# Tail V loads into freed K buffers and smaller V offsets in a grouped-query decode attention kernel

## Chip, cores, metric

One core of a Trainium2 chip. The time is device microseconds of one execution, quoted as a median of several. "TensorE" is the matrix engine (PE in the profile; PEld its weight loads), "ScalarE" is ACT, "VectorE" is DVE, "GpSimd" is POOL; SP is the engine that issues all loads. The "granted clock" is the share of TensorE's full clock that the profile records; in these traces it is 1.0 or 0.5 ("half clock") at any moment, and a mean over a run lies between (0.964 in the kernel before).

## The reference

One token of 32 query heads reads 8 K/V heads of 65,536 keys with 128 elements each, in bf16:

```python
B, Hq, Hkv, Sq, Sk, D = 1, 32, 8, 1, 65536, 128
k = jnp.repeat(k, Hq // Hkv, axis=1); v = jnp.repeat(v, Hq // Hkv, axis=1)
scores = jnp.einsum("bhqd,bhkd->bhqk", q, k) * D ** -0.5
p = softmax(scores, axis=-1)
out = jnp.einsum("bhqk,bhkd->bhqd", p, v)
```

K and V together are 268 MB, read once.

## The kernel before

A chunk is 8,192 keys (2 MB). Each head has 8 K chunks and 8 V chunks. For a K chunk, TensorE transposes 64 tiles into PSUM, the memory in which this kernel lets its results land ("TR"), VectorE evacuates (copies out) six and ScalarE two of its eight PSUM groups, and 64 score matmuls follow one chunk later ("QK"). ScalarE copies the scores out. After a head's last QK come its maximum and four exponentials on ScalarE (one for each query head), and only then can its V chunks be multiplied ("PV", 64 matmuls per chunk). An offset says how many K chunks of the next head pass before a head's first PV:

```python
    T=64, NK=4, NV=5,          # tiles per chunk, K buffers, V buffers
    DOFF=2, DOFF_LAST=1,       # offsets: heads 0-5, heads 6-7
...
        def merged(vdelay, vdelay_last):
            ...
            for (_, h, c) in kitems:
                lst.append((NCH * h + c, 0, ("K", h, c)))
            for (_, h, c) in vitems:
                d = vdelay_last if h >= H - 2 else vdelay
                lst.append((NCH * (h + 1) + c + d + 0.5, 1, ("V", h, c)))
            lst.sort(key=lambda x: (x[0], x[1]))
```

This one list orders both the loads and TensorE's work. A K load waits for the transposes of the K chunk four earlier, a V load for the PV five earlier.

ScalarE's program has the four exponentials in a row, between its evacuations:

```python
            for g_ in range(R):
                ac.activation(pview[:, g_, :], sview[:, g_, :], AF.Exp, ..., accum_out=...).then_inc(exp_done, 1)
```

## Time and profile before

| | before |
|---|---|
| time, median of 6 runs (range) | 662.66 us (658.25 to 668.54) |
| span of the profiled run | 660.0 us |
| TensorE busy | 601.2 us (91%), mean granted clock 0.964 |
| VectorE, ScalarE busy | 282.6 us, 198.6 us |
| transfers in the plateau (slices 5 to 36) | 423 to 427 GB/s |
| instruction fetches on the DMA engines (queue q8) | 97 packets, 1.59 MB |

The slices of the page cut the span into 40 parts. TensorE and the transfers both look full, so the busy shares alone can't say which of them sets the time; the waits can. The prediction shows these lines and reads them.

### The profile page before, as it was taken

The page shows a single profiled execution, that of the slowest core. Times are in us where ns is not written, and L with a number is a line of the kernel's source. Part 1 is how long each engine was busy: PE and PEld are TensorE (multiplying, and loading weights), DVE is VectorE, ACT ScalarE, POOL GpSimd, SP SyncE. Part 2 cuts the span into 40 slices and gives each one's busy share as a digit, 9 for nine tenths or more (in the row PEclk, how much of TensorE's full clock was granted, in tenths as well). Part 3 has the DMA queues.
Part 4 walks back from the last instruction along what each step waited for, and adds up shares of the span by engine and source line. Part 5 has one row for each costly group of instructions (what it writes and reads, how often), then busy time and mean ns, then how long its engine had stood idle before and what let it go on. Part 6 is the DMA issues. An engine that isn't in the chain of part 4 may idle for free.

```text
span 660.0 us, 25999 instructions
## 1 busy us (share of the span) xinstructions
PE 601.2 (91%) x12289; PEld 585.6 (89%) x12289; DVE 282.6 (43%) x491; ACT 198.6 (30%) x266; POOL 7.1 (1%) x22
## 2 busy tenths in 40 slices
PE   3889799889999999999999899999999999998998
PEld 3889699889989899898998889998899989898997
DVE  1767534344444435435434354354444444442300
ACT  1434522134222422226222162222522143221400
POOL 0000000000000000000000000000000000000000
PEclk9989798998999989999989999899999999998799
DMA  8999999999999999999999999999999999998694
GB/s 353 422 390 402 426 426 425 424 427 425 426 424 424 423 425 426 426 426 424 425 424 425 426 425 425 425 425 425 424 425 426 425 425 424 426 425 329 255 424 197
DMA packets 18621, 270.11 MB, mean 409 GB/s; under 512 B 2132, under 2 KB 2132, under 8 KB 2132
## 3 DMA queue, kind: packets, MB, share of 16 engines
q1 hardware_dynamic: 18516, 268.46, 96.5%
q8 instruction: 97, 1.59, 1.0%
q14 instruction: 8, 0.07, 0.0%
HBM read 268.44 MB, written 0.01 MB: 407 GB/s over the span
## 4 chain that ended last, share of the span: by engine, by line
PE 85%; issue 8%; ACT 3%; DMA 2%; DVE 1%; POOL 0%; POOLq 0%; DVEq 0%
PE trb L285 35%; PE pvb L327 35%; PE qkb L305 16%; ACT pts L445 2%; DMA vbuf<-in_v_dram 2%; ACT ktb L469 1%; DVE hpart L370 0%; ACT scs L421 0%; POOL hmaxa L250 0%; DVE hmax L377 0%; ACT negb L430 0%; DVE orows L400 0%; POOL ident L244 0%; POOL ident L242 0%; PE trb L264 0%
## 5 line engine op out<-in xcount | busy, mean ns | idle before, releaser
L360 DVE COPY ktb<-trb 128x1024 bf16<-128x1024 bf16 x384 | 237.9, 683 | 194.9 <-PE trb L285 193.6
L327 PE MATMUL pvb<-vbuf,pts 128*4 128x128 bf16 x4096 | 257.0, 226 | 19.6 <-issue 19.0
L327 PEld LDWEIGHTS pvb<-vbuf,pts 128*4 128x4 bf16 x4096 | 243.5, 88 | 24.2 <-issue 22.3
L285 PE MATMUL trb<-ident,kbuf 128*128 128x128 bf16 x4096 | 249.2, 222 | 17.0 <-issue 9.8
L285 PEld LDWEIGHTS trb<-ident,kbuf 128*128 128x128 bf16 x4096 | 234.9, 99 | 26.8 <-issue 12.6
L469 ACT ACTIVATE ktb<-trb 128x1024 bf16<-128x1024 bf16 x128 | 131.2, 1025 | 358.9 <-PE trb L285 358.9
L305 PE MATMUL qkb<-qT,ktb 128*128 128x4 bf16 x4096 | 113.8, 165 | 9.1 <-issue 9.1
L305 PEld LDWEIGHTS qkb<-qT,ktb 128*128 128x128 bf16 x4096 | 110.3, 96 | 10.2 <-issue 10.1
L370 DVE TENSOR_REDUCE hpart<-scs 128x4 f32<-128x256 f32 x64 | 38.7, 605 | 111.9 <-ACT scs L421 111.9
L445 ACT ACTIVATE pts<-scs,negb 128x512 bf16<-128x512 f32 x32 | 41.1, 1435 | 0.3
L421 ACT ACTIVATE scs<-qkb 128x256 f32<-128x256 f32 x64 | 24.5, 383 | 48.1 <-PE qkb L305 48.1
L400 DVE TENSOR_SCALAR orows<-pvb,rcol 4x128 bf16<-4x128 f32 x8 | 2.7, 339 | 57.4 <-PE pvb L327 57.4
L264 PE MATMUL trb<-ident,qsb 32*128 32x32 bf16 x1 | 0.2, 178 | 10.6 <-POOL ident L244 10.6
L264 PEld LDWEIGHTS trb<-ident,qsb 32*128 32x128 bf16 x1 | 0.1, 100 | 10.6 <-issue 10.6
L250 POOL PARTITION_ALL_REDUCE hmaxa<-hmax x8 | 3.0, 373 | 565.8 <-DVE hmax L377 565.8
L445 ACT ACTIVATION_READ_ACCUMULATOR pts<-scs,negb 128x1 f32 x32 | 8.2, 256 | 0.0
L430 ACT ACTIVATE negb<-hmaxa 128x4 f32<-128x4 f32 x8 | 1.6, 205 | 11.1 <-POOL hmaxa L250 11.1
L339 DVE CAST identf<-ident 4x4 f32<-4x4 bf16 x1 | 0.2, 158 | 10.5 <-POOL ident L244 10.5
L255 POOL PARTITION_ALL_REDUCE lsum<-rsum x8 | 3.4, 430 | 44.0 <-ACT pts L445 44.0
L411 ACT ACTIVATE dscr<-ident 128x1 f32<-128x1 bf16 x1 | 0.2, 202 | 8.5 <-POOL ident L244 8.5
L377 DVE TENSOR_REDUCE hmax<-hpart 128x4 f32<-128x32 f32 x8 | 1.7, 207 | 0.3
L411 ACT ACT_TABLE_LOAD x1 | 1.3, 1283 | 0.7 <-PEq L495 0.7
(11 smaller groups left out, 4.3 us busy)
## 6 DMA issues: line engine op xcount, KB each, us to landing
kbuf<-in_k_dram SPq DMA_DIRECT2D x64, 2048.0 KB, 20.6
vbuf<-in_v_dram SPq DMA_DIRECT2D x64, 2048.0 KB, 26.0
qsb<-in_q_dram SPq DMA_DIRECT2D x1, 8.0 KB, 1.7
out_dram<-orows SPq DMA_DIRECT2D x1, 8.0 KB
```

What stands on the lines that cost most here:

```text
L250: g.partition_all_reduce(hmaxa[:, h * R:(h + 1) * R], hmax[:, h * R:(h + 1) * R], P, bass.bass_isa.ReduceOp.max,).then_inc(hmaxa_rdy, 1)
L255: g.partition_all_reduce(lsum[:, h * R:(h + 1) * R], rsum[:, h * R:(h + 1) * R], P, bass.bass_isa.ReduceOp.add,).then_inc(lsum_rdy, 1)
L285: ins = pe.transpose(trb[bnk][:, (gti % TB) * P:(gti % TB + 1) * P], kv3[:, t, :], ident[:, :],)
L305: ins = pe.matmul(qkb[bnk][:, t * R:(t + 1) * R], lhsT=ktb[slot][:, t * P:(t + 1) * P], rhs=qT[:, h * R:(h + 1) * R], start=True, stop=True,)
L327: ins = pe.matmul(pvb[bnk][0:R, 0:D], lhsT=pts[pslot][:, tau * R:(tau + 1) * R], rhs=vv3[:, t, :], start=(tau == 0), stop=(tau == TPH - 1),)
L360: dv.tensor_copy(ktb[slot][:, j * TB * P:(j + 1) * TB * P], trb[bnk][:, :],).then_inc(tr_fre[bnk], 1)
L370: dv.tensor_reduce(hp[:, pslot, c, :], scs[pslot][:, c * T * R:(c + 1) * T * R].rearrange("p (t g) -> p g t", g=R), AX.X, ALU.max,).then_i ...
L377: dv.tensor_reduce(hmax[:, h * R:(h + 1) * R], hp[:, pslot, :, :].rearrange("p c g -> p g c"), AX.X, ALU.max,).then_inc(hmax_rdy, 1)
L400: dv.tensor_scalar(orows[:, h * D:(h + 1) * D], pvb[bnk][0:R, 0:D], rcol[:, h:h + 1], None, ALU.mult,).then_inc(pv_fre[bnk], 1)
L421: ac.activation(scs[pslot][:, qc * T * R:(qc + 1) * T * R], qkb[bnk][:, 0:T * R], AF.Copy,).then_inc(qk_fre[bnk], 1)
L445: ac.activation(pview[:, g_, :], sview[:, g_, :], AF.Exp, bias=negb[:, h * R + g_:h * R + g_ + 1], scale=scale, accum_out=rsum[:, h * R + ...
L469: ac.activation(ktb[slot][:, j * TB * P:(j + 1) * TB * P], trb[bnk][:, :], AF.Copy,).then_inc(tr_fre[bnk], 1)
```

## The change

The intent is to close the hole in the transfers near the end. Once no K is left to load, the K buffers that fall free take V chunks 0 to 3 of the last head, and both offsets shrink by one so that V comes earlier. Two further switches in the diff (FSPLIT, QKPV) are off and are cut here.

```diff
-    DOFF=2,
-    DOFF_LAST=1,
+    DOFF=1,
+    DOFF_LAST=0,
+    TAILK=1,
...
+    nkd = min(NK, NCH - 1) if TAILK else 0
+    for (_, h, c) in vitems:
+        if h == H - 1 and c < nkd:
+            kc_prev = NKC - NK + c
+            vdest[(h, c)] = ("k", kc_prev % NK, kc_prev)
+        else:
+            vb_idx[(h, c)] = cnt_vb
+            vdest[(h, c)] = ("v", cnt_vb % NV)
+            cnt_vb += 1
...   # SP, for a V chunk whose destination is a K buffer
+                    grp_last = kc_prev * GPB + (GPB - 1)
+                    sp.wait_ge(tr_full[grp_last % NTB], tr_full_after(grp_last))
+                    sp.dma_start(kbuf[kslot][:, :], src).then_inc(k_rdy[kslot], 16)
...   # TensorE reads V from there
+                    pe.wait_ge(k_rdy[kslot], 16 * (krdy_count(kslot, kc_prev) + vuses))
+                    vsrc = kbuf[kslot]
```

## The prediction

> **What bounds the kernel now.** The kernel streams 64 K chunks and 64 V chunks of 2 MB each. For each K chunk TensorE makes 64 transposes (L285) and 64 score matmuls (L305), for each V chunk 64 output matmuls (L327). Both streams leave on one queue, in the order in which TensorE uses them. I first read the page's slices, because 268 MB make the transfers the first suspect.

> ```profile
> PE   3889799889999999999999899999999999998998
> ...
> PEclk9989798998999989999989999899999999998799
> DMA  8999999999999999999999999999999999998694
> GB/s 353 422 390 402 426 426 425 424 427 425 426 424 424 423 425 426 426 426 424 425 424 425 426 425 425 425 425 425 424 425 426 425 425 424 426 425 329 255 424 197
> ```

> The transfers run flat at about 425 GB/s, except in slices 1 to 4 and in slices 37 and 38 (594 to 627 us), the hole that the change is aimed at. The windows view of 595 to 630 us reads 338, 334, 311, 298, 324, 170 and 305 GB/s in steps of 5 us. Against 425 that lacks (87+91+114+127+101+255+120) x 5 us = 4.5 MB, or 10.5 us of transfer. A naive reading makes that the gain. So the second view is the one of waits: does TensorE ever wait for a transfer?

> ```profile
> PE pvb L327 <- issue: 19.0, 20, 1.3
> ...
> PE trb L285 <- issue: 9.8, 16, 1.4
> ...
> PE qkb L305 <- issue: 9.1, 13, 1.2
> ...
> PE trb L285 <- ACT ktb L469: 6.7, 4, 3.7
> ...
> PE pvb L327 <- DMA vbuf<-in_v_dram: 0.5, 1, 0.5
> ```

> The columns are total us, times, longest. After its start TensorE waited for data once, for 0.5 us. Its idle time is 10.6 us before the first transpose, 37.9 us of short "issue" gaps, 6.7 us for ScalarE's evacuations and this 0.5 us. Together with 601.2 us busy that is 656.9 of the 660.0 us span; 2.4 us of what is left is the store at the end (last matmul 657.55). So TensorE is the bound and the queue runs ahead of it: K chunk 63 was issued at 571.58 us, a K chunk lands 20.6 us after issue (median), and its transposes started only at 610.58 us, some 18 us after it lay there. The margin isn't large: from one head's exponentials to the next (149.29, 226.97, 304.55 us) TensorE took 77.6 us for 8 pairs, 9.70 us a pair, while two chunks at 425 GB/s take 2 x 2.097 / 0.425 = 9.87 us.

> The third view is TensorE's timeline of the tail (start, duration):

> ```profile
> 614.16 1.64 PE L305 MATMUL qkb<-qT,ktb 128*128 128x4 bf16 x60
> 616.73 0.25 PE L305 MATMUL qkb<-qT,ktb 128*128 128x4 bf16 x4 [0.92 <-issue]
> 617.17 1.85 PE L305 MATMUL qkb<-qT,ktb 128*128 128x4 bf16 x64 [0.20 <-issue]
> 618.95 34.35 PE L327 MATMUL pvb<-vbuf,pts 128*4 128x128 bf16 x576
> 653.80 3.73 PE L327 MATMUL pvb<-vbuf,pts 128*4 128x128 bf16 x64 [0.50 <-DMA vbuf<-in_v_dram]
> ```

> After the last scores TensorE multiplies ten V chunks without a hole: nine in 34.35 us, 0.50 us for the last chunk, then that one. The hole in the transfers is inside TensorE's own busy time. Also to be seen: the first two of the ten (V of head 6) hide the exponentials of head 7.

> The fourth view is what those exponentials cost; the chain of waits shows it bare at head 0, where no V work lies in between:

> ```profile
> 66.27 0.39 ACT scs L421
> ...
> 66.69 0.61 DVE hpart L370
> ...
> 67.32 0.22 DVE hmax L377
> ...
> 67.67 0.40 POOL hmaxa L250
> ...
> 68.09 0.21 ACT negb L430
> ...
> 69.53 3.92 ACT pts L445 x7
> 73.45 0.86 ACT ktb L469
> ```

> The last score matmul ended at 66.25, the exponentials at about 73.45: 7.2 us from a head's last scores to its probabilities. I take the last matmul of head 7 (618.95) as a check: there ScalarE's last exponential starts at 624.74 and takes 1.42, so 626.2, again 7.2 us.

> [...] head 0's stall of 3.71 us and head 1's of only 1.19 us (150 to 154 us) are both followed by half clock, in the column before the DMA share:

> ```profile
> 77.00:80.50 3.50, 3.50 (x38) 3.50 (x35) 2.59 (x4) 0.38 (x1) 0.00 (x0) 0.50 1.01 431
> ...
> 155.60:159.00 3.40, 3.40 (x58) 3.38 (x55) 0.84 (x4) 0.61 (x2) 0.00 (x0) 0.50 0.99 414
> ```

> In such a stretch 64 matmuls take 5.3 us instead of 3.67, so a stall costs its own length plus about 1.7 us per stretch; after head 0's stall there were two stretches (73.7 to 80.5 us). [...] the evacuation at 73.45 waited behind four exponentials. [...]

> **The change part by part.**
> FSPLIT=1 and QKPV=0 switch their new code off: nothing.
> TAILK: V chunks 0 to 3 of head 7 go into the four K buffers as the transposes of K 60 to 63 release them. V chunks 4 to 7 need only V chunks 3 to 6 of head 6 to be consumed. No load of head 7 waits any more for an output matmul of head 7, or for one behind its exponentials. Estimate of the new tail, from the end of K 63's transposes (T): at the latest five chunks are then still to be issued, about 2 + 5 x 4.93 = 27 us, while TensorE's last chunk starts about 3.3 + 7.2 + 7 x 3.6 = 36 us after T. The last load gets about 9 us of slack. What it takes off the path is the 0.5 us wait.
> DOFF 2 to 1: V of heads 0 to 5 moves one pair earlier. The order of instructions on TensorE shows that head 0's first V multiply comes after K 9 instead of K 10, and that from a head's last scores to its first V multiply there is now one pair instead of two. One pair is enough: the transposes in it need ScalarE's evacuation, which stands behind the exponentials, so the wait is paid there as before (3.7, 1.2, 1.2, 0.6 us at four heads). Change: 0.
> DOFF_LAST 1 to 0, head 6: after the last scores of head 6 come V chunk 7 of head 5 and then at once chunk 0 of head 6, with no transposes between. 3.6 us of work against 7.2 us leaves a new stall of 3.6 us. In the kernel before, a whole pair lay there and head 6 had no stall of this kind (its exponentials ended at 547.1, TensorE went on). The half clock after it adds 1.7 to 3.4 us. Sum 5.3 to 7.0; one gap of 0.6 us (37.9 us over 64 pairs) may fall inside it. About 6.
> DOFF_LAST, head 7: after the last scores one V chunk of head 6 instead of two. Now the end follows 7.2 us of exponentials, then 8 chunks of 3.6 us = 28.8, plus 1.7 to 3.4 us of half clock: 37.7 to 39.4 us after the last scores. Before it was 657.55 - 618.95 = 38.6 us, with one chunk (3.6 us) more in it, which now lies ahead of the last scores. So 2.7 to 4.4 more, 0.5 us for the vanished load wait already in it. About 3.
> The sum is -0 (transfers) + 6 (head 6) + 3 (head 7) = +9 us at full effect. The clock part is uncertain, since half clock also follows chance gaps and part of it is there in the tail already; I shade to +7: 662.66 + 7 = 669.7.

> **The rivals.**
> (a) The transfers bind, the hole is real, and filling it gives up to 10.5 us: 652. For it: the flat 425 GB/s, 9.87 against 9.70 us a pair, and the last load landing 0.04 us before its matmul. Against: one wait of 0.5 us in 650.
> (b) The earlier V makes TensorE wait for loads in the middle, as the lead of some 18 us is lost. Queue and TensorE have the same order in both kernels, so the lead stays; against it also that V starts earlier in the slices where the queue has room. If so, 680.
> (c) The stalls come but the half clock doesn't, or it takes the place of half clock already there: +4, 667.
> (d) The gaps called "issue", 49 of them, shift with the new order. They depend on how the instructions fall, and could move the total by some 5 us either way.

> **Range and chances.** The six runs before spread from 658.25 to 668.54, so the median itself is good to some 3 us. With +2 to +12 for the stalls I say 661 to 676. Over 2% slower (above 675.9) needs both stalls with full half clock and bad luck in (d): 0.10. Over 2% faster (below 649.4) needs more than rival (a) can give: 0.04.

> **What would show each step.** Right: the slices lose the hole at 594 to 627 us, the last load lands some 9 us before the last matmul starts, and TensorE has no wait for DMA; two new waits of 2 to 4 us of L382 (the output matmul) on ScalarE's exponentials, one near 555 us and one about 35 us before the end, each with half clock after it. Wrong: no such waits, or the last matmul still waiting for its load, or a total number of half-clock stretches far below the 13 of the kernel before.

## More of the kernel before

In the PV multiply the probabilities are the stationary operand and V moves (in the page the weight load is 128x4, the matmul 128x128):

```python
                    ins = pe.matmul(
                        pvb[bnk][0:R, 0:D],
                        lhsT=pts[pslot][:, tau * R:(tau + 1) * R],
                        rhs=vv3[:, t, :], ...)
```

## The result

| | before | after |
|---|---|---|
| median (range; runs) | 662.66 us (658.25 to 668.54; 10 runs) | 671.04 us (664.86 to 673.91; 5 runs) |
| span of the profiled run | 660.0 us | 670.0 us |
| TensorE busy, mean clock | 601.2 us, 0.964 | 609.0 us, 0.954 |

The ratio is 1.0123, with a 95% interval from 1.0065 to 1.018. A ratio is the mean time of one kernel's fast runs over that of the other's fast runs of the same rounds, so it isn't quite the ratio of the medians. The change makes the kernel about 8 us slower, within the class "within 2%".

The page of the changed kernel, slices:

```profile
PE   3988799899999999999999989999999997999998
...
PEclk9998799988899999888899999999899988989889
DMA  8999999999999999999999999999999999998690
GB/s 354 424 409 426 427 423 428 425 423 426 425 426 423 425 425 425 425 425 426 424 423 416 404 424 418 425 426 421 429 423 425 425 424 407 425 399 315 269 410 5
```

The hole near the end hasn't gone. It reads 399, 315, 269 in slices 36 to 38, because loads into K buffers wait for transposes just as K loads do (SP's four such waits are 40.5 us together). But the last slice moves 5 GB/s instead of 197: the transfers are over well before TensorE is. In the trace the last V chunk landed at 654.6 us and was multiplied from 663.9 us, so it lay there for 9.3 us. In the kernel before, it landed as TensorE reached it.

The waits of TensorE in the changed kernel (total us, times, longest):

```profile
PE pvb L382 <- issue: 24.9, 23, 3.6
...
PE trb L333 <- issue: 8.2, 11, 1.3
PE qkb L353 <- issue: 7.3, 11, 1.0
...
PE trb L333 <- ACT ktb L523: 6.6, 3, 4.3
```

TensorE's wait for a load (0.5 us) is gone. In its place the longest "issue" wait of the PV multiply went from 1.3 to 3.6 us. TensorE's timeline (start, duration, then in brackets the idle time before) shows where, first at head 6:

```profile
548.87 3.73 PE L382 MATMUL pvb<-vbuf,pts 128*4 128x128 bf16 x64
556.17 5.30 PE L382 MATMUL pvb<-vbuf,pts 128*4 128x128 bf16 x64 [3.57 <-issue]
561.41 3.75 PE L333 MATMUL trb<-ident,kbuf 128*128 128x128 bf16 x64
```

then at the end:

```profile
629.91 5.36 PE L382 MATMUL pvb<-vbuf,pts 128*4 128x128 bf16 x64
637.22 16.08 PE L382 MATMUL pvb<-kbuf,pts 128*4 128x128 bf16 x256 [1.95 <-issue]
653.13 14.46 PE L382 MATMUL pvb<-vbuf,pts 128*4 128x128 bf16 x256
```

The label "issue" says that the profile found no releaser. ScalarE's timeline of the same moment finds it:

```profile
554.65 1.42 ACT L499 ACTIVATE pts<-scs,negb 128x512 bf16<-128x512 f32 x1
555.82 0.25 ACT L499 ACTIVATION_READ_ACCUMULATOR pts<-scs,negb 128x1 f32 x1
```

The last exponential of head 6 ended at 556.07 and the PV began at 556.17. The 64 matmuls behind the stall took 5.30 us instead of 3.67: half clock (the granted clock was 1.00 during the stall, 0.50 from 556.1 to 559.4 us, then 1.00 again). At the end, the chunk ahead of the stall already ran at half clock (5.36 us), which left 1.95 us to wait, and the four chunks behind it took 16.08 us where four undisturbed ones took 14.46.

The span grew by 10.0 us: TensorE's busy time by 7.8 us (half clock: 18 stretches of 3.41 us in its trace, 14 in the one before) and its idle time (span less busy) from 58.8 to 61.0, by 2.2. The two new stalls alone are 5.5 us, so the other gaps became smaller by about 3.3 us. That is the first sign that the gaps aren't a fixed cost.

### The profile page after: what moved, and what is told of

It reads as the page before. It is cut to its first block, busy times and chain, and to the rows that moved or that the text cites.

```text
span 670.0 us, 25999 instructions
## 1 busy us (share of the span) xinstructions
PE 609.0 (91%) x12289; PEld 593.0 (89%) x12289; DVE 282.6 (42%) x491; ACT 199.1 (30%) x266; POOL 7.1 (1%) x22
## 4 chain that ended last, share of the span: by engine, by line
PE 88%; issue 8%; ACT 2%; DVE 0%; POOL 0%; POOLq 0%; DVEq 0%
PE pvb L382 38%; PE trb L333 35%; PE qkb L353 15%; ACT pts L499 2%; ACT ktb L523 0%; DVE hpart L425 0%; ACT scs L475 0%; POOL hmaxa L295 0%; DVE hmax L432 0%; ACT negb L484 0%; DVE orows L454 0%; POOL ident L289 0%; POOL ident L287 0%; PE trb L309 0%; DVE qT L396 0%
## 5 line engine op out<-in xcount | busy, mean ns | idle before, releaser
L382 PE MATMUL pvb<-vbuf,pts 128*4 128x128 bf16 x3840 | 250.8, 230 | 23.1 <-issue 23.0
L382 PEld LDWEIGHTS pvb<-vbuf,pts 128*4 128x4 bf16 x3840 | 236.5, 90 | 28.2 <-issue 26.8
L333 PEld LDWEIGHTS trb<-ident,kbuf 128*128 128x128 bf16 x4096 | 233.5, 99 | 25.2 <-issue 10.8
L382 PE MATMUL pvb<-kbuf,pts 128*4 128x128 bf16 x256 | 16.1, 231 | 1.9 <-issue 1.9
L382 PEld LDWEIGHTS pvb<-kbuf,pts 128*4 128x4 bf16 x256 | 15.9, 90 | 2.1 <-issue 2.1
L309 PE MATMUL trb<-ident,qsb 32*128 32x32 bf16 x1 | 0.2, 181 | 10.6 <-POOL ident L289 10.6
L309 PEld LDWEIGHTS trb<-ident,qsb 32*128 32x128 bf16 x1 | 0.1, 97 | 10.6 <-issue 10.6
L394 DVE CAST identf<-ident 4x4 f32<-4x4 bf16 x1 | 0.2, 157 | 10.5 <-POOL ident L289 10.5
```

Of the source, the lines that this page charges most:

```text
L333: ins = pe.transpose(trb[bnk][:, (gti % TB) * P:(gti % TB + 1) * P], kv3[:, t, :], ident[:, :],)
L382: ins = pe.matmul(pvb[bnk][0:R, 0:D], lhsT=pts[pslot][:, tau * R:(tau + 1) * R], rhs=vv3[:, t, :], start=(tau == 0), stop=(tau == TPH - 1),)
```

## The experiments

Twelve kernels ran, all with correct results (one of the 20 timed runs of k was over 1.5% above its fastest, which counts as slow, and isn't in its ratio). Kernels of one job share their runs of the kernel before.

### a: the buffer reuse alone

```diff
-    DOFF=1, DOFF_LAST=0,
+    DOFF=2, DOFF_LAST=1,      # TAILK=1 stays
```

> The changed kernel with both offsets put back (2 and 1), so that only the reuse of K buffers for the tail V loads is left. My theory (TensorE is the bound, the hole in the transfers is hidden behind it): ratio to the kernel before 0.999, between 0.995 and 1.003; no wait on probabilities in head 6 or at the end; the last load lands well before its matmul. Rival (the transfers bind in the tail, and only the new stalls cover the gain): 10 us faster, ratio 0.985.

Measured: 664.65 us median against 661.30, ratio 1.0041 (1.0004 to 1.0079). The 10 us gain of the rival isn't there. The number is slightly above my range; the mean granted clock of its six runs was 0.957 against 0.964 of the kernel before in the same job. Run b holds the same reuse and shows no loss, so I don't read a cost of the reuse out of it; why this run is 0.4% slower stays open.

### b: reuse and the smaller offset for heads 0 to 5

```diff
-    DOFF_LAST=0,
+    DOFF_LAST=1,
```

> The changed kernel with the last offset put back to 1; K buffer reuse and offset 1 for heads 0 to 5 stay. My theory (the whole loss is the last offset): ratio to before 1.000, between 0.995 and 1.005. Rival (the earlier V loads of heads 0 to 5 cost something, by lost lead or by gaps that moved): ratio 1.005 to 1.012.

Measured: 661.74 us, ratio 1.0002 (0.9961 to 1.0043). As expected. Reuse and offset 1 together cost nothing and gain nothing; putting back the last offset alone removes the whole loss.

### c: both offsets without the reuse

```diff
-    TAILK=1,
+    TAILK=0,
```

> The changed kernel without the reuse of K buffers; both new offsets stay. My theory: the new stalls alone make the loss, the tail loads have slack even so (the last V load is issued at about 650 us when chunk 2 of head 7 is done, lands about 658, and is needed at about 664): ratio to before 1.012, between 1.006 and 1.018, as the changed kernel. Rival (the reuse pays for a part of the new offsets): slower than the changed kernel, ratio 1.02 or more, with the last matmuls waiting for their loads.

Measured: 671.40 us, ratio 1.0158 (1.0111 to 1.0204), with no wait of TensorE for a load in its profile. The loss is there without the reuse. The intervals of this run and of the changed kernel (1.0065 to 1.018) overlap, so the reuse's own share isn't resolved.

### d: a larger dose of the stall

```diff
-    DOFF=1,
+    DOFF=0,
```

> The changed kernel with offset 0 for heads 0 to 5 too, a larger dose: each head's first V multiply then stands right behind its last score multiply, so seven heads show the bare 7.2 us. My theory with half clock after each stall: heads 1 to 5 add 5 x (7.2 + 3.4) = 53 us less the 6 us of stalls on ScalarE's evacuations that go, head 0 adds 3, head 6 adds 5: 671 + 55 = 726, ratio to before 1.095, between 1.075 and 1.11. Rival without the half clock: 671 + 5 x 7.2 - 2 + 3 + 4 = 712, ratio 1.074 or less. Rival that the lead of the transfers absorbs stalls: ratio below 1.04.

Measured: 700.81 us, ratio 1.0603 (1.0559 to 1.0647). The stalls came as foreseen, seven of 7.2 to 7.3 us. One of them in TensorE's timeline:

```profile
165.78 4.41 PE L382 MATMUL pvb<-vbuf,pts 128*4 128x128 bf16 x48 [7.27 <-ACT pts L499]
```

The total missed both of my sums, 726 and 712. The page shows the span up by 29.5 us on the changed kernel's, TensorE's busy time unchanged (608.8 against 609.0) and its idle time up by 29.7. Two things in my sums were wrong. First, half clock cost nothing where it fell inside the stall: the mean clock went from 0.954 to 0.929, the busy time didn't rise. In the trace 99.2 us are at half clock, 37.3 of them while TensorE stood still; in the changed kernel it is 61.6 and 3.1. Second, the stalls took gaps with them. Seven stalls of 7.2 us in place of those of 4.3 us (head 0, ScalarE's evacuation) and 3.6 us (head 6) are 43 us more, but the idle time rose by 30 only. In the timeline behind the stall that ended at 249.59 us, TensorE then ran to 280.15 us without one gap (behind all seven, 16 to 57 us without one over 0.3 us), while the kernel before had 49 "issue" gaps in 650 us, one every 13. So something seems to fall behind while TensorE runs and to catch up while it stands; run j gives it a name.

### e and f: one stall at a time

```diff
-                d = vdelay_last if h >= H - 2 else vdelay
+                # e: only the stall at head 6
+                d = (0 if c < 4 else 1) if h == H - 2 else (0 if h == H - 1 else vdelay)
+                # f: only the stall at the end
+                d = (1 if c < 4 else 0) if h == H - 2 else (0 if h == H - 1 else vdelay)
```

> The changed kernel, but chunks 4 to 7 of head 6 keep offset 1, so that two V chunks of head 6 are left over for the time of head 7's exponentials; only the stall at head 6 stays. My theory (two separate stalls): one wait of about 3.6 us near 553 us and none at the end; 3.6 + 1.7 us of half clock, less up to 2 us of gaps called issue that it takes the place of: +4 us, ratio to before 1.006, between 1.002 and 1.010. Rival (the loss is all at the end of the kernel): ratio below 1.002.

Measured: 666.86 us against 664.02, ratio 1.0048 (1.0007 to 1.0090); one stall of 3.57 us at head 6, none at the end. TensorE's timeline:

```profile
552.14 5.36 PE L382 MATMUL pvb<-vbuf,pts 128*4 128x128 bf16 x64 [3.57 <-issue]
```

> The changed kernel, but chunks 0 to 3 of head 6 keep offset 1 and only chunks 4 to 7 have offset 0, so that one V chunk of head 6 is left over for head 7's exponentials; only the stall at the end stays. My theory: no wait near 553 us, one of about 2 us before head 7's first V multiply, +3 us, ratio to before 1.004, between 1.000 and 1.008. Rival (the loss is all at head 6): ratio below 1.000. The excesses of this run and the one before should add up to that of the changed kernel, 0.012.

Measured: 665.95 us, ratio 1.0040 (0.9991 to 1.0088); no stall at head 6 beyond 1.2 us on ScalarE's evacuation, and 1.68 us before head 7's first PV (the view was cut off at 640 us):

```profile
631.37 8.81 PE L382 MATMUL pvb<-kbuf,pts 128*4 128x128 bf16 x155 [1.68 <-issue]
```

The excesses add up to 0.0088, inside the changed kernel's interval. So the loss seems to come from both places, some 3 us each (0.0048 and 0.0040 of 664 us are 3.2 and 2.7). The traces show each stall; the times are less sure, as e's interval is 0.5 to 6.0 us and f's, -0.6 to 5.8 us, takes in zero.

### g and h: exponentials spread between evacuations, with and without the reuse

ScalarE now issues two exponentials, an evacuation, two exponentials, an evacuation (at head 0: none, two, one, one). Offsets 2 and 1.

```diff
-            for g_ in range(R):
-                ac.activation(... AF.Exp ...)
+            expq.extend((one, g_) for g_ in range(R))
+            plan.extend([0, 2, 1, 1] if h == 0 else [2, 2])
...
                 for j in range(GPB):             # ScalarE's evacuations
+                    if plan:
+                        pop(plan.pop(0))
```

> A version meant to beat both: K buffer reuse with the old offsets, and ScalarE's four exponentials of a head are no longer issued in a row but two before each of the next two evacuations (at head 0 none, two, one, one), so that the transposes don't wait for an evacuation behind four exponentials. My theory (TensorE is the bound): the 6.7 us of waits on ScalarE's evacuations and the half clock after them (5 stretches of 1.6 us) go, up to 14 us, of which the gaps called issue take some back: 6 to 10 us faster, ratio to before 0.988, between 0.980 and 0.995. Rival (the transfers bind soon, 268.4 MB at 425 GB/s are 632 us and the start and the end add some 16): ratio not below 0.985. Rival (all of it comes back as issue gaps): ratio 0.998 or more.

Measured: 660.29 us against 664.02, ratio 0.9964 (0.9922 to 1.0005). The waits on ScalarE's evacuations (6.7 us before) are gone from the profile, yet the gain is about 2 us, not clear of noise, where I expected 6 to 10. The rival that it comes back elsewhere is nearly right, and the bound of the other, that the transfers bind soon (not below 0.985), is kept too. The profiled run's TensorE was busy for 609.9 us instead of 601.2, at a clock of 0.951; but this was the slowest of g's six runs (663.68 us), and the others had clocks of 0.959 to 0.969.

> The same version without the reuse of K buffers. My theory: as long as TensorE is the bound the reuse is worth nothing, so equal to the version with it within 2 us; the last V chunk's load is issued only when chunk 2 of head 7 has been multiplied, which leaves no slack, so a wait of up to 2 us for the last load may show. Rival (with a faster TensorE the transfers bind, and the hole at the end costs): 5 us or more slower than the version with reuse.

Measured: 660.78 us, ratio 0.9978 (0.9930 to 1.0026), the same as g within the noise. Its profiled run had a high clock (0.974), and in it the loads at the end do bind. TensorE's timeline:

```profile
638.10 3.73 PE L382 MATMUL pvb<-vbuf,pts 128*4 128x128 bf16 x64 [1.65 <-DMA vbuf<-in_v_dram]
643.00 3.73 PE L382 MATMUL pvb<-vbuf,pts 128*4 128x128 bf16 x64 [1.17 <-DMA vbuf<-in_v_dram]
647.86 3.73 PE L382 MATMUL pvb<-vbuf,pts 128*4 128x128 bf16 x64 [1.13 <-DMA vbuf<-in_v_dram]
652.73 3.73 PE L382 MATMUL pvb<-vbuf,pts 128*4 128x128 bf16 x64 [1.14 <-DMA vbuf<-in_v_dram]
```

The four starts are 4.9 us apart, the time of a 2 MB load at 425 GB/s, and the four waits are 5.1 us together, more than the 2 us that I allowed. The g profile, with the reuse, has none. This pair alone doesn't show that the reuse removes such waits, as g's profiled run was a slow one and TensorE came later there; j and k below make the same comparison.

### j, k, m: a TensorE with much less array work

If TensorE's array is the bound, less array work must help. Here V is the stationary operand and the four columns of probabilities move, so a chunk takes 1.6 us (1.61 from 306.18 us on in the chain of waits of run j) instead of 3.7 at full clock (3.67 in the kernel before). The result, which then comes out transposed, is scaled by VectorE and turned once at the end.

```diff
                     ins = pe.matmul(
-                        pvb[bnk][0:R, 0:D],
-                        lhsT=pts[pslot][:, tau * R:(tau + 1) * R],
-                        rhs=vv3[:, t, :],
+                        pvb[bnk][:, 0:R],
+                        lhsT=vv3[:, t, :],
+                        rhs=pts[pslot][:, tau * R:(tau + 1) * R],
...
+        pe.transpose(trb[0][0:HR, 0:P], oT[:, :], ident[:, :]).then_inc(ot_sem, 1)
```

> TensorE made faster without touching the loads: in the output multiply V is the stationary operand and the four columns of probabilities move (the form that the score multiply has, 64 in 1.6 us instead of 3.7), with the result transposed once at the end; offsets 2 and 1 and no reuse of K buffers, as in the kernel before. If TensorE was the bound, this drops by the 2.1 us of 64 chunks until the transfers bind: 268.4 MB at 425 GB/s = 632 us, about 8 us for the start and 5 for the end: 645, ratio to before 0.973, between 0.965 and 0.983, slices at 425 GB/s to the end and TensorE waiting for loads. Rival (the transfers bound the kernel before as well): ratio 0.99 or more.

Measured: 661.41 us against 661.47, ratio 0.9999 (0.9979 to 1.0019). A clean miss of my theory; the number is that of the rival (0.99 or more), to which I come back below. The page and the waits of this kernel:

```profile
PE 539.5 (82%) x12290; PEld 531.8 (81%) x12290; DVE 295.3 (45%) x476; ACT 198.8 (30%) x266; POOL 7.1 (1%) x22
```

```profile
PE pvb L382 <- issue: 50.3, 23, 3.3
...
PE trb L333 <- issue: 38.5, 25, 3.3
```

Busy time fell by 62 us, and idle time rose by as much: the "issue" gaps from 37.9 to 90.4 us (with 1.6 us before score matmuls), the waits for the last loads from 0.5 to 7.9 us. The fall in busy time hides two changes. The PV group fell by 140 us (257.0 to 117.0), but the transposes, which the edit doesn't touch, rose by 87 us, as the mean granted clock fell from 0.964 to 0.778. Their lines in the pages of the kernel before and of j (busy us and mean ns after the bar):

```profile
L285 PE MATMUL trb<-ident,kbuf 128*128 128x128 bf16 x4096 | 249.2, 222 | 17.0 <-issue 9.8
...
L333 PE MATMUL trb<-ident,kbuf 128*128 128x128 bf16 x4096 | 336.0, 260 | 48.0 <-issue 38.5
```

The gaps aren't waits for loads: in the trace, after the first six K chunks, K and V chunks lay in their buffers for some 8 to 21 us before TensorE reached them, until the last five V chunks. Nor do the gaps stand at chunk borders, where the waits for loads are; they stand in the middle of one, here after 11 of 64 transposes:

```profile
307.65 0.77 PE L333 MATMUL trb<-ident,kbuf 128*128 128x128 bf16 x11
310.45 5.79 PE L333 MATMUL trb<-ident,kbuf 128*128 128x128 bf16 x53 [2.02 <-issue]
```

A packet of the instruction queue began at 308.12 us and took 1.1 us, and TensorE went on 1.2 us after it had ended. Most gaps end like this one: of the 53 TensorE gaps over 0.5 us in this trace, 46 end between 0.8 and 2.0 us after a packet of that queue ended, and in the kernel before 37 of 42 (the others are mostly the waits on ScalarE and for the last loads). With a packet about every 6.7 us, chance would put some 18% of them into a window of 1.2 us. Counting is stricter than chance: if TensorE's instructions (matmuls, weight loads, semaphore instructions) are numbered in order, 507 of the 525 "issue" gaps over 0.5 us in the 14 traces stand before number 192 or 193 past a multiple of 256, so at one place of a block of 256; among the other 18 are the stalls on the exponentials. I read this as TensorE standing in these gaps for its next instructions. What the kernels before, after, a to h, j and k have in common is the number of TensorE's instructions: 12,289 or 12,290 matmuls with as many weight loads, fetched in 97 packets of 16,384 bytes, one for about 257 instructions (24,911 stand in the trace of the kernel before).

The rival, that the transfers bound the kernel before as well, isn't out by this. From slice 5 to 36 the slices read 418 to 429 GB/s in j, 423 to 427 in the kernel before, and the last load landed at 653.8 and 655.9 us. In this reading TensorE waits for instructions and not for loads, but in the traces the fetches come later while loads run. From TensorE's entry into a block to the start of the next block's fetch, the median is 3.8 us where the loads moved 418 GB/s or more in this time (1,162 blocks of the 14 traces) and 1.0 us where they moved less than 50 (16 blocks). A block with a gap at its end took 6.3 us at full transfers (median of 417). A pair of chunks is 389 instructions, 1.52 blocks, which makes 9.6 us (an estimate) of the 9.70 us that TensorE took for a pair in the kernel before. So the transfers may set TensorE's pace by way of the fetches, and j can't tell this from a supply that is slow by itself.

> The same faster TensorE with all that the change brings (offsets 1 and 0, reuse of K buffers). My theory: with the transfers as the bound, TensorE's stalls on the exponentials lie in slack, so the loss of 0.012 is gone: equal to the run before it within 0.003. Whether the reuse gains anything then depends on whether the hole near the end exists there: if V buffers are freed as fast as they fill there is no hole, and I expect none. Rival (the change is what the transfers needed): 5 to 10 us faster than the run before it, ratio below 0.965.

Measured: 660.33 us, ratio 0.9967 (0.9941 to 0.9992). The change doesn't cost anything here; against j it is equal or about 2 us faster (the intervals of the two just overlap). In j the last V chunks cost TensorE 7.9 us of waits for loads; here there is none, and a stall of 5.56 us on head 7's exponentials stands there instead. The hole I didn't expect is there in both (246 and 260 GB/s in slice 38).

> The run before it, and the loads of V chunks 0 and 1 of head 0 are issued right after K chunks 5 and 7, as their buffers are empty then and the transfers have room while TensorE works through K alone. If the transfers bind, filling the start's hole (slices 1 to 4 of the kernel before lack about 5 us of transfer, 2 of them before the first byte) gives 2 to 4 us: ratio to before 0.968, between 0.960 and 0.975. Rival (the hole at the start isn't on the path): equal to the run before it.

Measured: 660.58 us, ratio 0.9970 (0.9947 to 0.9993). Slices 3 and 4 went from 392 and 410 GB/s in k to 427 and 426, so the hole at the start is filled, and the time is that of k. The hole at the start isn't on the path, as the rival said.

### n: more instructions, little array work

```diff
-                for t in range(T):
+                for t in [tt // 2 for tt in range(2 * T)]:   # each score matmul twice
                     ins = pe.matmul(qkb[bnk][:, t * R:(t + 1) * R], ...)
```

> The kernel with V stationary (old offsets, no reuse), in which every score multiply is issued twice into the same place. In that kernel the loads lay ready 10 to 20 us before TensorE came to them and the array worked 61 us less than in the kernel before, yet the time did not move; the one thing that stayed is the number of TensorE's instructions, 24,578 in 97 fetches of 256, of which a fetch began every 6.5 us, a tenth of them closer than 6.0. My theory now: the supply of instructions sets TensorE's pace while the transfers run. Then 8,192 more instructions in 32 more fetches at 6.0 to 6.6 us add 190 to 210 us: about 860 us, ratio to before 1.29, between 1.20 and 1.35, with the period of the fetches still near 6.3 us. Rival (the array is the bound, as I predicted): 64 x 1.6 = 102 us more array work fill the 108 us of gaps, up to 700, ratio 1.06 or less. Rival (the transfers bind): 661, ratio 1.00.

Measured: 804.45 us against 663.41, ratio 1.2098 (1.2002 to 1.2193); 143 us more than j. From the page of the kernel before, the instruction queue's line (packets, MB, share of the 16 DMA engines):

```profile
q8 instruction: 97, 1.59, 1.0%
```

and from the page of this run:

```profile
PE 685.3 (85%) x16386; PEld 676.3 (84%) x16386; DVE 298.5 (37%) x476; ACT 198.8 (25%) x266; POOL 7.1 (1%) x22
...
GB/s 364 370 227 352 424 410 394 383 380 345 357 400 335 330 388 299 343 334 297 358 289 378 288 345 277 341 281 346 314 354 328 382 424 369 295 317 315 207 250 284
...
q1 hardware_dynamic: 18528, 268.46, 84.0%
q8 instruction: 129, 2.11, 1.0%
```

Neither rival holds: both allow no more than 1.06. The transfers have room now (337 GB/s on average), and V chunk 8 lay ready 36 us before its use, so no load was in the way before the last chunks. The gaps again end with fetches, 52 of 58. From TensorE's first to its last matmul, the fetches compare with the array's work like this; the work is an estimate at full clock from 64 transposes in 3.68 us, scores in 1.58, and PV in 3.67 or 1.6:

| kernel | array work for all chunks | fetches | work per fetch | time per fetch |
|---|---|---|---|---|
| before | 64 x 8.93 = 572 us | 97 | 5.9 us | (657.5 - 10.6) / 97 = 6.67 us |
| j | 64 x 6.86 = 439 us | 97 | 4.5 us | (658.4 - 10.8) / 97 = 6.68 us |
| n | 64 x 8.44 = 540 us | 129 | 4.2 us | (801.3 - 10.8) / 129 = 6.13 us |

Work fell by almost a third, and the time per fetch stayed within a tenth. For the kernel before and j the last column says no more than that both took the same time for as many instructions; n is the test. The ratio is at the low end of my range, and my central figure, 860 us, was too high, because the period became shorter: 22 of n's 128 fetches follow the one before in less than 5 us, 2 of 96 in the kernel before, and n's transfers, 337 GB/s on average against 409, may have left the fetches more room.

The run isn't as clean as I meant it to be. The sum of TensorE's gaps is the same in j and n (108 and 105 us in the trace), and the 143 us stand in the page as busy time: 685.3 against 539.5. The score group accounts for 105 us of it (112.3 to 217.4), and the rest is mostly transposes at half clock (mean 278 ns against 260; mean granted clock 0.718 against 0.778). The gaps don't bring it about alone: 35 of n's 62 drops of the clock follow a window that was at least 95% busy, with four-column matmuls for the most part. A reader who takes the gaps for a fixed 105 us could get most of n from the added work; j contradicts that, as there the gaps grew when the work shrank.

What stays open is how much of the 6.7 us a fetch is supply alone, how much half clock, and how far the transfers set both. No run had fewer instructions, or fewer loads in flight.

## Why the prediction was right

The time (671.04 against 669.7 predicted), the range and the class held. Step by step:

1. **The hole is hidden behind TensorE's own work.** Shown. Run a has the reuse without the new offsets and gains nothing, and m fills another hole and gains nothing.
2. **The smaller offset for heads 0 to 5 changes nothing.** Shown by b, 1.0002.
3. **Two new stalls on the exponentials, 3.6 us at head 6 and about 2 to 4 us at the end.** Shown: 3.57 and 1.95 us. Runs e and f have one of them each, run b none, and the loss goes along.
4. **The sum, +6 and +3.** Its sign and size held: 8 us, against 9 at full effect and 7 after shading. The single terms aren't resolved: run e measures 3.2 us for head 6 (0.5 to 6.0), f 2.7 us for the end (-0.6 to 5.8). The half clock came as foreseen, 5.30 us for the chunk behind head 6's stall and 16.08 instead of 14.46 for the four at the end. The mis-sized term is the fixed gaps: I let a stall absorb one gap of 0.6 us, while the other gaps lost 3.3 us in the profiled pair, and run d shows 16 to 57 us without one behind a stall. That the shading, made for the clock, took off about as much is luck.
5. **"The slices lose the hole."** Wrong. The loads into K buffers wait for transposes, and the hole stays at 269 GB/s. The other half of that step, about 9 us of slack for the last load, held: 9.3 us. (The 2 us ahead of the five loads in that estimate were my allowance; the 8 KB load of q took 1.7 us from issue to landing.)
6. **"So TensorE is the bound."** True as far as the waits show: it didn't wait for loads, save at the very end. The lead was read wrongly, though: K chunk 63 didn't lie there for 18 us. I took the median time to landing; this chunk landed at 600.63 us, 29 us after its issue, and lay there for 9.9 us, and the last V chunk for 0.04 us. And I took its array time and its gaps for two separate sums. Run j shows that array time alone doesn't set the pace: 62 us less busy time moved nothing, idle time grew by as much, 52.5 us of it in "issue" gaps, most of which end with instruction fetches. It doesn't show that the transfers weren't the bound behind the fetches. Run n fits this (143 us for 8,192 more matmuls with their weight loads) without proving it alone. While the transfers ran at 418 GB/s or more, TensorE's pace was near that of its instruction fetches (9.6 us a pair, the estimate above, against 9.70), and array work, half clock and short waits traded against "issue" gaps. That would also be why g got back only 2 us for 6.7 us of waits removed.
7. **Rival (d), gaps that shift by chance.** Present throughout. The changed kernel's runs spread from a span of 662.8 us at a clock of 0.969 to 671.9 us at 0.949. How much of the 7.8 us of busy time in the profiled pair belongs to the two stalls and how much to chance isn't settled.

The fastest versions tried, g, k and m, are all about 660 us: 0.3 to 0.4% under the kernel before and 1.6% under the changed kernel (671.04 to 660.33, in different jobs). Only for k and m does the interval exclude 1.

## What to carry to other kernels

Before filling a hole in the transfers, ask the waits whether anyone stood still because of it. When V work is moved ahead of a softmax, count the engine work that remains between the last score and the first use of the probabilities: it has to cover the whole chain (here 7.2 us), or the difference becomes a stall (here 3.6 us of work left one of 3.57). And when an engine shows many short gaps with no releaser, count its instructions before shortening them: if the gaps stand at one place of a block of 256 (here 507 of 525) and grow as the work shrinks (37.9 to 90.4 us), the supply of instructions is worth relieving first (no run here tried it). A matmul made short cost something here: with four moving columns instead of 128 in PV, the mean granted clock fell from 0.964 to 0.778, and the transposes took 87 us more.
